# Seven block products for two projections of the second mixture stage

## Chip, cores and metric

The kernel runs on one core of one Trainium2 chip, as one program. The metric is device time in microseconds (us). The kernel before takes 781.18 us (median of three runs, 780.84 to 781.45).

## What is computed

Three parts follow one another on 1536 tokens (2 x 768) of width 512: an attention in which a query sees only keys of its own hash bucket, a mixture in which each token goes through one of eight experts, and a second mixture without experts. The change lies in the last:

```python
def _moe2_ref(x, w_a, w_b, w_out):      # x: 1536 x 512; w_a, w_b: 512 x 1536; w_out: 1536 x 512
    a = x @ w_a
    b = x @ w_b
    return (a * b @ w_out).astype(np.float32)
```

The three weights come as 64-bit floats (the array `w2in`) and are converted to 32 bits on the chip.

## The kernel before

Attention and experts fill the first 465 us. They leave the second stage's input y transposed in SBUF: 512 channels as four blocks of 128 partitions (index d) by 1536 tokens. y is kept as two tiles, `y_h` (rounded to fp32r) and `y_l` (what the rounding left), and weights are split in the same way, so every product of two numbers takes three matmuls: h by h, h by l, l by h (`mm3`).

The stage goes through 1536 hidden units in 12 chunks f of 128, for two halves c of the tokens (768 each), and each half in two steps hf of 384 tokens. The list `steps` has 48 entries (c, f, hf). A step's `ab` (L954) makes a and b in two PSUM banks, `aba` and `abb`: 2 x 4 channel blocks x 3 matmuls, the weights standing, 384 tokens streaming. ScalarE copies a (L965), VectorE multiplies b by it (L966), ScalarE rounds the product to `gh` (L969) and VectorE subtracts to `gl` (L970). `outp` (L975) multiplies `gh` and `gl` by the w_out block: three blocks of 128 tokens, three matmuls of 512 columns each, added up in six PSUM banks `acc0` to `acc5` over the 12 chunks. After the last chunk ScalarE or VectorE copies each bank to an `osb` tile and GpSimd scatters its rows to the output (L420). `outp` runs one step behind `ab`.

The order of the instructions on each engine is the order of the program: everything stands under `tc.manual_schedule()`, there is no planner, each engine takes its own instructions in order, and semaphores make them wait for each other.

Weights: `w2_load` (L802, on SP) brings chunk m as 1.5 MB of raw words; `w2_a` (ScalarE, L488) and `w2_b` (VectorE, L493, L495, L499) convert each third (w_a, w_b, w_out; 512 columns each) to a 32-bit tile `t2`; `w2_c` splits it: h on ScalarE (L826), l on GpSimd (L827). Chunk numbers m run from 0 to 23, the second dozen being the same weights again for the later tokens. Chunks 2 to 9 stay in SBUF as `t2` tiles (the pool `keep`); 0, 1, 10 and 11 are loaded and converted a second time as 12, 13, 22 and 23. `conv_pre` and `conv_post` place this work around each step: before a step the splits for the next one, after it the conversions.

Of the kernel before, what the change touches and what calls it, by code (L numbers as in the profile page):

```python
# [19 lines left out]
S, D, NB, NH = 768, 64, 2, 8  # L20
NT = 6
N, DM, E, FF, F2 = 1536, 512, 8, 1024, 1536
C = 224
KEEP = range(2, 10)
# [9 lines left out]
def attn_moe_kernel(ctx: ExitStack, tc: tile.TileContext, xin, cst, projd, wblk, wmoe, w2in, out):  # L34
    nc = tc.nc
    PE, ACT, DVE, POOL = nc.tensor, nc.scalar, nc.vector, nc.gpsimd

    const = ctx.enter_context(tc.tile_pool(name="const", bufs=1))
    dram = ctx.enter_context(tc.tile_pool(name="dram", bufs=1, space=DRAM))
# [6 lines left out]
    big = ctx_a.enter_context(tc.tile_pool(name="big", bufs=1))  # L46

    cs = const.tile([128, CW], F32, name="cs")
    wb = const.tile([128, NH, 160], F32, name="wb")
    wl = const.tile([128, 80], F32, name="wl")  # L50
    pst = const.tile([128, 64], F32, name="pst")
# [4 lines left out]
    idtab = dram.tile([N, 2], F32, name="idtab")  # L56
    ones = const.tile([128, 128], BF16, name="ones")
    tri = const.tile([128, 128], BF16, name="tri")
    lg = const.tile([128, 12, 16], F32, name="lg")
# [427 lines left out]
    def f64_hi(r, t):  # L487
        ACT.activation(t, r.bitcast(F32)[:, :, 1], ACTF.Copy, scale=float(2.0**-112))  # L488

    def f64_f32(r, t, x, parts=(0, 1, 2)):  # L490
        tu = t.bitcast(U32)
        if 0 in parts:
            DVE.tensor_scalar(out=x, in0=tu, scalar1=0x80000000, scalar2=None, op0=ALU.bitwise_and)  # L493
        if 1 in parts:
            DVE.scalar_tensor_tensor(  # L495
                out=x, in0=r[:, :, 0], scalar=29, in1=x, op0=ALU.logical_shift_right, op1=ALU.bitwise_or
            )
        if 2 in parts:
            DVE.scalar_tensor_tensor(out=tu, in0=tu, scalar=3, in1=x, op0=ALU.logical_shift_left, op1=ALU.bitwise_or)  # L499
# [94 lines left out]
    with tc.manual_schedule():  # L594
# [30 lines left out]
        for n in (2, 1):  # L625
            part, half = half[:n], half[n:]
# [22 lines left out]
            out=tokc.bitcast(I32)[:, :, 0], in0=cs[:, C_TOK:C_TOK + 12], scalar1=-float(E * C), scalar2=None, op0=ALU.add  # L649
# [10 lines left out]
        for g in range(NG):  # L660
            h, t = divmod(g, NT)
# [132 lines left out]

        R2, W2 = {}, {}

        T2, X2, keep = {}, {}, []

        def known(m):
            return m - 12 in KEEP  # L800

        def w2_load(m):  # L802
            if m < 24 and not known(m):
                R2[m] = r2.tile([128, F2, 2], U32, tag="r2", name="r2")
                nc.sync.dma_start(out=R2[m], in_=w2in[m % 12].bitcast(U32).rearrange("p (n two) -> p n two", two=2))

        def w2_a(m, i):
            if m < 24 and not known(m):
                if m in KEEP:
                    T2[m, i] = keep[0].tile([128, 512], F32, tag=f"t{m}{i}", name="t2")  # L810
                else:
                    T2[m, i] = c2.tile([128, 512], F32, tag="t2", name="t2", bufs=6)
                f64_hi(R2[m][:, i * 512:(i + 1) * 512], T2[m, i])

        def w2_b(m, i, parts=(0, 1, 2)):
            if m < 24 and not known(m):
                if 0 in parts:
                    X2[m, i] = c2.tile([128, 512], U32, tag="x2", name="x2")
                f64_f32(R2[m][:, i * 512:(i + 1) * 512], T2[m, i], X2[m, i], parts)

        def w2_c(m, i):
            if m < 24:
                h = s2.tile([128, 512], F32R, tag=f"h2{i}", name=f"h2{i}")
                l = s2.tile([128, 512], F32R, tag=f"l2{i}", name=f"l2{i}")
                t = T2[m - 12 if known(m) else m, i]
                ACT.activation(h, t, ACTF.Copy)  # L826
                POOL.tensor_tensor(out=l, in0=t, in1=h.bitcast(F32), op=ALU.subtract)  # L827
                W2[m, i] = h, l

        XG, HT, Y = {}, {}, {}  # L830

# [115 lines left out]
        ctx_m.close()  # L947
        ctx_w.close()

        keep.append(ctx_2.enter_context(tc.tile_pool(name="keep", bufs=1)))  # L950
# [4 lines left out]
        def ab(c, f, hf):  # L955
            p = [pa.tile([128, 512], F32, tag="ab" + "ab"[i], name="ab" + "ab"[i]) for i in range(2)]
            t0 = c * 768 + hf * 384
            first = (c, f, hf) == (0, 0, 0)
            order = [(i, d) for k in range(2) for i in range(2) for d in (2 * k, 2 * k + 1)]
            for i, d in order if first else sorted(order):  # L960
                    wh, wl = W2[c * 12 + f, i]
                    w = slice(d * 128, (d + 1) * 128)
                    mm3(p[i][:, :384], wh[:, w], wl[:, w], y_h[:, d, t0:t0 + 384], y_l[:, d, t0:t0 + 384], d == 0, d == 3)
# [11 lines left out]
        def outp(c, f, hf):  # L975
            wh, wl = W2[c * 12 + f, 2]
            h, l = G.pop((c, f, hf))
            for j in range(3):
                i = hf * 3 + j
                if f == 0:  # L980
                    acc[i] = pa.tile([128, 512], F32, tag=f"acc{i}", name=f"acc{i}")
                w = slice(j * 128, (j + 1) * 128)
                PE.matmul(acc[i], h[:, w], wh, start=(f == 0), stop=False)
                PE.matmul(acc[i], h[:, w], wl, start=False, stop=False)
                PE.matmul(acc[i], l[:, w], wh, start=False, stop=(f == 11))
                if f == 11:
                    o = gp.tile([128, DM], F32, tag="o", name="osb", bufs=7)
                    k = c * 6 + i
                    if i % 2 == 0:
                        ACT.activation(o, acc.pop(i), ACTF.Copy, scale=cc[:, k:k + 1])  # L990
                    else:
                        DVE.tensor_scalar(out=o, in0=acc.pop(i), scalar1=cc[:, k:k + 1], scalar2=None, op0=ALU.mult)
                    scatter(
                        scat_o, out=out, out_offset=bass.IndirectOffsetOnAxis(ap=ids.bitcast(I32)[:, k, 0:1], axis=0),
                        in_=o, in_offset=None,
                    )

        def conv_pre(m, hf):
            if hf == 0:
                w2_c(m, 2)  # L1000
            else:
                w2_c(m + 1, 0)
                w2_c(m + 1, 1)
# [9 lines left out]
                w2_a(m + 2, 0)  # L1013
                w2_a(m + 2, 1)

        conv = [(m, hf) for m in range(25) for hf in range(2)]
        steps = [(m // 12, m % 12, hf) for m, hf in conv[:48]]
        steps[-3], steps[-2] = steps[-2], steps[-3]
        for n in range(48):
            conv_pre(*conv[n + 1])  # L1020
            ab(*steps[n])
            if n:
                outp(*steps[n - 1])
            conv_post(*conv[n + 1])
        outp(*steps[-1])
        ctx_2.close()
        overflow()

# [57 lines left out]
```

## Time and profile before

| | us |
|---|---|
| median of three runs | 781.18 |
| the profiled execution | 780.29 |
| its span, first to last instruction | 778.5 |
| TensorE busy (matmuls) | 750.7 (96%) |
| weight loads busy (beside matmuls) | 644.4 (83%) |
| VectorE busy | 484.5 (62%) |
| ScalarE busy | 413.0 (53%) |
| GpSimd busy | 229.6 (29%) |
| mean granted TensorE clock | 0.984 |

The profiled execution's time lies 1.8 us above its span and 0.9 us under the median of the runs. Shares of the span are means over stages of different kinds, so they say little about one of them; a stage is read by its own stretch of time. Matmuls overlap: one of 384 columns is on record with 0.34 us, while the next starts 0.175 us later, so starts are compared and not durations. In the rows PE is TensorE, PEld its weight loads, DVE VectorE, ACT ScalarE, POOL GpSimd.

### The profile page before, as it was taken

How to read it: one execution, taken by the hardware profiler on the slowest of the kernel's cores; microseconds unless marked ns; L12 is line 12 of the kernel's file. 1: busy time of each engine (PE TensorE's matmuls, PEld its weight loads, DVE VectorE, ACT ScalarE, POOL GpSimd, SP SyncE). 2: the span in 40 equal slices, each digit the busy share in tenths (PEclk: the TensorE clock that was granted, in tenths of full speed). 3: DMA queues.
4: the chain of work that ended last, by engine and by line, in shares of the span. 5: the costliest groups of instructions: out<-in, count | busy, mean ns of one | idle time of the engine just before them, and what ended most of it. 6: DMA issues, size and time to landing. Idle time of an engine off the chain costs nothing. (4 is left out here: it accounts for less than half of the span.)

```text
span 778.5 us, 13032 instructions
## 1 busy us (share of the span) xinstructions
PE 750.7 (96%) x4911; PEld 644.4 (83%) x4912; DVE 484.5 (62%) x862; ACT 413.0 (53%) x768; POOL 229.6 (29%) x226
## 2 busy tenths in 40 slices
PE   7899999999999989799999999999999999999995
PEld 5566666667666789799999999999999999999995
DVE  5777777788786767466667875666676731111442
ACT  4777777777777435355556654444434432322331
POOL 3223233222534382500000003233333443333223
PEclk8999999999999989899999999999999999999998
DMA  7257241212201055876796552424233430000002
GB/s 241 91 198 254 95 166 56 102 63 69 96 32 59 28 203 180 112 223 216 216 375 216 185 164 82 162 82 162 92 153 111 174 122 1 1 1 1 0 1 84
DMA packets 28916, 94.75 MB, mean 122 GB/s; under 512 B 5984, under 2 KB 9392, under 8 KB 26800
## 3 DMA queue, kind: packets, MB, share of 16 engines
q1 hardware_dynamic: 26176, 87.35, 34.1%
q0 software_dynamic: 2304, 6.31, 2.2%
q8 instruction: 41, 0.67, 0.4%
q10 hardware_dynamic: 368, 0.20, 0.1%
q14 instruction: 27, 0.22, 0.1%
HBM read 79.62 MB, written 13.12 MB: 119 GB/s over the span
## 5 line engine op out<-in xcount | busy, mean ns | idle before, releaser
L827 POOL TENSOR_TENSOR l<-t,h 128x512 fp32r<-128x512 f32 x72 | 95.7, 1334 | 324.9 <-ACT h L826 321.5
L163 DVE TENSOR_REDUCE mm<-s 128x1 f32<-128x768 f32 x96 | 91.8, 956 | 33.9 <-PE s L158 30.3
L474 DVE TENSOR_TENSOR wl<-wr,wh 128x1024 fp32r<-128x1024 f32 x62 | 75.9, 1224 | 53.5 <-ACT wh L473 49.8
L184 PEld LDWEIGHTS tp<-cs,p 128*128 128x128 f32 x576 | 63.1, 142 | 55.4 <-ACT p L171 35.4
L171 ACT ACTIVATE p<-s,sb 128x768 f32<-128x768 f32 x96 | 95.2, 992 | 19.9 <-PE tp L184 10.1
L966 DVE TENSOR_TENSOR a_sb<-abb,a_sb 128x384 f32<-128x384 f32 x48 | 26.8, 558 | 121.8 <-PE abb L858 103.4
L473 ACT ACTIVATE wh<-wr 128x1024 fp32r<-128x1024 f32 x64 | 67.9, 1061 | 57.2 <-PE y L885 49.5
L188 ACT ACTIVATE pt<-tp 128x384 f32<-128x384 f32 x144 | 67.1, 490 | 45.3 <-PE tp L184 44.1
L826 ACT ACTIVATE h<-t 128x512 fp32r<-128x512 f32 x72 | 44.4, 629 | 87.0 <-DVE t L499 80.5
L184 PE MATMUL tp<-cs,p 128*128 128x128 f32 x576 | 84.2, 283 | 6.4 <-ACT p L171 4.6
L157 PE MATMUL s<-tk,tq 76*128 76x384 f32 x192 | 73.7, 384 | 2.3 <-DVE tq L134 2.3
L856 PE MATMUL h<-xh,wh 128*128 128x224 f32 x256 | 72.9, 285 | 2.5 <-ACT wh L473 1.5
L885 PE MATMUL y<-hl,wh 128*128 128x224 f32 x256 | 72.1, 282 | 2.1 <-DVE hl L870 2.1
L858 PE MATMUL h<-xh,wl 128*128 128x224 f32 x256 | 71.5, 279 | 2.6 <-DVE wl L474 2.3
L884 PE MATMUL y<-hh,wh 128*128 128x224 f32 x256 | 71.7, 280 | 1.2 <-ACT hh L869 1.2
L857 PE MATMUL h<-xl,wh 128*128 128x224 f32 x256 | 71.3, 279 | 0.3 <-DVE xl L411 0.3
L886 PE MATMUL y<-hh,wl 128*128 128x224 f32 x256 | 71.2, 278 | 0.0
L199 PE MATMUL av<-pt,v 128*64 128x384 f32 x360 | 71.1, 503 | 0.0
L158 PE MATMUL s<-bk,bq 128*128 128x384 f32 x192 | 65.5, 341 | 0.0
L856 PE MATMUL aba<-y_h,h 128*128 128x384 f32 x192 | 65.0, 339 | 0.3 <-ACT a_sb L965 0.3
L856 PE MATMUL abb<-y_h,h 128*128 128x384 f32 x192 | 65.1, 339 | 0.0
L857 PE MATMUL aba<-y_l,h 128*128 128x384 f32 x192 | 64.5, 336 | 0.2 <-DVE y_l L892 0.2
(161 smaller groups left out, 1789.4 us busy)
## 6 DMA issues: line engine op xcount, KB each, us to landing
wr<-wmoe SPq DMA_DIRECT2D x64, 512.0 KB
r<-w2in SPq DMA_DIRECT2D x16, 1536.0 KB
x<-xin SPq DMA_DIRECT2D x30, 384.0 KB
xr<-zero SPq DMA_DIRECT2D x13, 512.0 KB
xg<-xr SPq DMA_DIRECT2D x14, 256.0 KB
v<-xin SPq DMA_DIRECT2D x16, 192.0 KB
wb<-wblk SPq DMA_DIRECT2D x1, 640.0 KB
x<-xin SPq DMA_DIRECT2D x3, 192.0 KB
```

The source lines that it names most:

```text
L157: PE.matmul(p[:, c, :384], T[h, 0][:76, qs], T[h, 1][:76, sl], start=True, stop=False)
L163: DVE.tensor_reduce(out=m[:, 1:2], in_=st[g][:, :, :384], axis=AX.XY, op=ALU.min)
L171: ACT.activation(p.rearrange("p (c n) -> p c n", c=2), st.pop(g)[:, :, :384], ACTF.Exp, scale=scl.pop(g), bias=nbs.pop(g), accum_out=sums[ ...
L184: PE.transpose(ps[:, j * 128:(j + 1) * 128], pt_[g][:, k * 128:(k + 1) * 128], ident)
L474: eng.tensor_tensor(out=l, in0=r, in1=h.bitcast(F32), op=ALU.subtract)
L827: POOL.tensor_tensor(out=l, in0=t, in1=h.bitcast(F32), op=ALU.subtract)
L856: PE.matmul(ps, wh, xh, start=first, stop=False)
L857: PE.matmul(ps, wh, xl, start=False, stop=False)
L858: PE.matmul(ps, wl, xh, start=False, stop=last)
L884: PE.matmul(p, wh[:, w], h, start=(f == 0 and d % 2 == 0), stop=False, skip_group_check=True)
L885: PE.matmul(p, wh[:, w], l, start=False, stop=False, skip_group_check=True)
L886: PE.matmul(p, wl[:, w], h, start=False, stop=(f == 7), skip_group_check=True)
```

## The change

For the later tokens (c = 1) and chunks 0 to 10, `seven` takes the place of four `ab`-like groups of products. It takes a and b of both token halves as one product of 2 x 2 blocks. The weight blocks are A11, A12 (w_a, lower and upper 256 channels) and A21, A22 (w_b); the blocks of y are its lower and upper 256 channels by two groups of 384 tokens. Seven products of sums and differences of blocks replace eight products of blocks. Each of the seven has two channel blocks x 3 = 6 matmuls of 384 columns.

- The sums and differences of y (t1 to t4, with h and l: `TH`, `TL`) are made once by `t_work`, in six portions on VectorE and ScalarE in steps 17 to 22 of the earlier half.
- The sums and differences of the weights (s1 to s4) are made by `s_work` on VectorE, one chunk ahead. `part` and `piece` split each of the seven weight operands (128 x 256): h on ScalarE, l on GpSimd.
- The products go to the two banks by turns. Between them, `fill` places one third of an `outp` of the chunk before, and `side` the next chunk's weight work. Copies and sums of banks (p1, u2, c11, u3, c22, c21, c12) are on ScalarE and VectorE.
- The last chunk runs `ab` and `outp` as before, in another order: `ab`, what is pending, `ab`, both `outp`.
- The pool `keep` goes. `w2_b` stores each converted tile to DRAM (`w32`, on SP's queue), and `t2_load` reads the tiles back for chunks 12 to 23. Nothing is converted twice.
- In the earlier half w_a and w_b are split in pieces of 256 columns instead of 512.
- `osb` has 5 buffers instead of 7; three small tiles move to another pool.

```diff
-        def known(m):
-            return m - 12 in KEEP
...
+        def t2_load(m):
+            if m < 24:
+                for i in range(3):
+                    nc.sync.dma_start(out=t2_tile(m, i), in_=w32[m - 12][:, i * 512:(i + 1) * 512])
...
         def w2_b(m, i, parts=(0, 1, 2)):
-            if m < 24 and not known(m):
+            if m < 12:
                 if 0 in parts:
                     X2[m, i] = c2.tile([128, 512], U32, tag="x2", name="x2")
                 f64_f32(R2[m][:, i * 512:(i + 1) * 512], T2[m, i], X2[m, i], parts)
+                if 2 in parts:
+                    nc.sync.dma_start(out=w32[m][:, i * 512:(i + 1) * 512], in_=T2[m, i])
...
+        def piece(key, src):
+            p = s2.tile([128, 2, 256], F32R, tag="pc", name="pc", bufs=11)
+            ACT.activation(p[:, 0], src, ACTF.Copy)
+            POOL.tensor_tensor(out=p[:, 1], in0=src, in1=p.bitcast(F32)[:, 0], op=ALU.subtract)
+            PCS[key] = p
...
+            return [
+                [whole(t3, lo_d, n2), whole(t1, lo_d, n1)],
+                [tt(t1, t3, t1), whole(t2, hi_d, n2)],
+                [tt(t3, t2, t3), tt(t2, t2, t1), hi(2)],
+                [tt(t4, yh[:, hi_d, n1], t2), tt(t4, t4, yl[:, hi_d, n1], ALU.add), hi(1), hi(0)],
+                [low(2), low(1), hi(3)],
+                [low(0), low(3)],
+            ]
...
+            if k == 0:
+                DVE.tensor_tensor(out=new("s1"), in0=a_part(m, "21"), in1=a_part(m, "22"), op=ALU.add)
+                DVE.tensor_tensor(out=new("s2"), in0=SW["s1"], in1=a_part(m, "11"), op=ALU.subtract)
+            elif k == 1:
+                DVE.tensor_tensor(out=new("s3"), in0=a_part(m, "11"), in1=a_part(m, "21"), op=ALU.subtract)
+            else:
+                DVE.tensor_tensor(out=new("s4"), in0=a_part(m, "12"), in1=SW["s2"], op=ALU.subtract)
+
+        ORDER = ("11", "s2", "12", "s3", "s1", "22", "s4")
...
+            def finish(hf, a, b):
+                DVE.tensor_tensor(out=b, in0=a, in1=b, op=ALU.mult)
...
+                ACT.activation(h, b, ACTF.Copy)
+                DVE.tensor_tensor(out=l, in0=b, in1=h.bitcast(F32), op=ALU.subtract)
+                G[1, f, hf] = h, l
+
+            x, y = bank(0), bank(1)
+            product(x, m, "11", *y_part(lo_d, n1), True)
+            p1 = sb("p1")
+            ACT.activation(p1, x, ACTF.Copy)
+            fill(0)
+            side(0)
+            product(y, m, "s2", TH[1], TL[1], True)
+            u2 = add(sb("u2"), y, p1)
+            fill(1)
+            side(1)
+            product(x, m, "12", *y_part(hi_d, n1), False)
+            c11 = sb("c11")
+            ACT.activation(c11, x, ACTF.Copy)
+            fill(2)
+            side(2)
+            product(y, m, "s3", TH[2], TL[2], False)
+            u3 = add(sb("u3"), y, p1)
+            fill(3)
+            side(3)
+            x = bank(0)
+            product(x, m, "s1", TH[0], TL[0], True)
+            c22 = add(sb("c22"), x, u3)
+            fill(4)
+            side(4)
+            product(y, m, "22", TH[3], TL[3], False)
+            c21 = add(sb("c21"), y, p1)
+            finish(0, c11, c21)
+            fill(5)
+            side(5)
+            product(x, m, "s4", *y_part(hi_d, n2), False)
+            c12 = add(sb("c12"), x, u2)
+            finish(1, c12, c22)
+            side(6)
...
+            def side(k):
+                if k == 0:
+                    w2_c(m, 2)
+                if f < 10:
+                    if k < 3:
+                        s_work(m + 1, k)
+                    part(m + 1, ORDER[k])
...
+                if k == 6:
+                    t2_load(m + 2)
...
+        w2_c(23, 2)
+        ab(1, 11, 0)
+        while pend:
+            outp(*pend.pop(0))
+        ab(1, 11, 1)
+        outp(1, 11, 0)
+        outp(1, 11, 1)
```

## Rows read from the trace of the kernel before

**Rows 1.** Busy time in two stretches of one chunk each, the first in the earlier half of the stage, the second in the later. Columns: stretch and its length in us, then busy us (and instructions) of PE, PEld, DVE, ACT and POOL, the granted clock, the DMA share and GB/s.

```profile
527.57:540.10 12.53, 12.53 (x68) 11.78 (x67) 8.37 (x13) 5.41 (x10) 3.99 (x4) 1.00 0.35 127
664.54:677.07 12.53, 12.53 (x68) 11.78 (x67) 2.24 (x4) 3.72 (x7) 3.81 (x3) 1.00 0.00 1
```

**Rows 2.** Instructions in order of time, TensorE, from the matmuls of `aba` to those of the next step. Columns here and in all rows in order of time: start us, duration us, engine, line, operation, output and inputs, shape; in brackets the idle time before it and who ended it.

```profile
655.27 0.33 PE L856 MATMUL aba<-y_h,h 128*128 128x384 f32 x1
655.27 0.19 PEld L857 LDWEIGHTS aba<-y_l,h 128*128 128x128 f32 x1
...
655.44 0.34 PE L857 MATMUL aba<-y_l,h 128*128 128x384 f32 x1
...
657.37 0.34 PE L856 MATMUL abb<-y_h,h 128*128 128x384 f32 x1
...
659.47 0.39 PE L983 MATMUL acc<-h,gh 128*128 128x512 f32 x1
...
661.54 0.33 PE L856 MATMUL aba<-y_h,h 128*128 128x384 f32 x1
```

**Rows 3.** In order of time: ScalarE's copy of `aba` and the first matmul that writes the bank again, at step 20 to 21 and at the start of the later half.

```profile
597.22 0.47 ACT L965 ACTIVATE a_sb<-aba 128x384 f32<-128x384 f32 x1
...
598.30 0.33 PE L856 MATMUL aba<-y_h,h 128*128 128x384 f32 x1
...
623.29 0.47 ACT L965 ACTIVATE a_sb<-aba 128x384 f32<-128x384 f32 x1
...
623.82 0.45 PE L856 MATMUL aba<-y_h,h 128*128 128x384 f32 x1 [0.29 <-ACT a_sb L965]
...
624.10 0.34 PE L857 MATMUL aba<-y_l,h 128*128 128x384 f32 x1
```

**Rows 4.** In order of time: at 474 and 654 operations that follow one another on one engine without needing each other, at 659 and 660 what follows the last matmul of a step.

```profile
474.38 0.56 DVE L970 TENSOR_TENSOR gl<-a_sb,gh 128x384 fp32r<-128x384 f32 x1 [0.59 <-ACT gh L969]
...
474.85 0.42 DVE L493 TENSOR_SCALAR x<-t 128x512 uint32<-128x512 uint32 x1
...
654.07 0.53 ACT L969 ACTIVATE gh<-a_sb 128x384 fp32r<-128x384 f32 x1 [2.22 <-DVE a_sb L966]
...
654.50 1.14 ACT L826 ACTIVATE h<-t 128x512 fp32r<-128x512 f32 x2
...
659.30 0.34 PE L858 MATMUL abb<-y_h,l 128*128 128x384 f32 x1
...
659.74 0.56 DVE L966 TENSOR_TENSOR a_sb<-abb,a_sb 128x384 f32<-128x384 f32 x1 [4.55 <-PE abb L858]
...
660.33 0.53 ACT L969 ACTIVATE gh<-a_sb 128x384 fp32r<-128x384 f32 x1 [2.22 <-DVE a_sb L966]
...
660.90 0.56 DVE L970 TENSOR_TENSOR gl<-a_sb,gh 128x384 fp32r<-128x384 f32 x1 [0.59 <-ACT gh L969]
```

**Rows 5.** Groups of instructions by line and shape: the two operations on 256 columns. Columns: line, engine, operation, tiles, shapes, count, busy us, mean ns, idle time before.

```profile
L368 POOL TENSOR_TENSOR xh<-x_all,xh 128x256 fp32r<-128x256 f32 x1 | 0.7, 737 | 0.4 <-ACT xh L367 0.4
L367 ACT ACTIVATE xh<-x_all 128x256 fp32r<-128x256 f32 x1 | 0.4, 421 | 3.4 <-DVE x_all L247 3.4
```

**Rows 6.** In order of time: VectorE and GpSimd side by side, at three places.

```profile
425.43 1.22 DVE L474 TENSOR_TENSOR wl<-wr,wh 128x1024 fp32r<-128x1024 f32 x1 [0.22 <-ACT wh L473]
...
426.00 1.80 POOL L827 TENSOR_TENSOR l<-t,h 128x512 fp32r<-128x512 f32 x1 [102.30 <-ACT h L826]
...
426.57 1.78 DVE L495 SCALAR_TENSOR_TENSOR x<-r,x 128x512 uint32<-128x512 uint32 x1
...
606.37 0.63 ACT L826 ACTIVATE h<-t 128x512 fp32r<-128x512 f32 x1 [1.92 <-DVE t L499]
...
606.71 0.69 DVE L495 SCALAR_TENSOR_TENSOR x<-r,x 128x512 uint32<-128x512 uint32 x1
...
607.08 1.47 POOL L827 TENSOR_TENSOR l<-t,h 128x512 fp32r<-128x512 f32 x1 [3.62 <-ACT h L826]
...
607.50 1.60 DVE L499 SCALAR_TENSOR_TENSOR t<-t,x 128x512 uint32<-128x512 uint32 x1
...
609.90 1.29 POOL L827 TENSOR_TENSOR l<-t,h 128x512 fp32r<-128x512 f32 x1 [1.35 <-ACT h L826]
...
610.24 0.56 DVE L966 TENSOR_TENSOR a_sb<-abb,a_sb 128x384 f32<-128x384 f32 x1 [1.14 <-ACT a_sb L965]
```

**Rows 7.** In order of time: the end of the program, from the last step's `outp` to the last scatters.

```profile
766.00 0.39 PE L983 MATMUL acc<-h,gh 128*128 128x512 f32 x1
...
766.87 0.53 ACT L969 ACTIVATE gh<-a_sb 128x384 fp32r<-128x384 f32 x1 [2.22 <-DVE a_sb L966]
...
768.95 0.75 DVE L992 TENSOR_SCALAR osb<-acc,cc 128x512 f32<-128x512 f32 x1 [0.96 <-PE acc L985]
...
769.63 0.69 ACT L990 ACTIVATE osb<-acc,cc 128x512 f32<-128x512 f32 x1 [2.23 <-PE acc L985]
...
769.98 0.96 POOL L420 DMA_INDIRECT out<-osb,ids  x1 [4.37 <-DVE osb L992]
...
772.50 0.96 POOL L420 DMA_INDIRECT out<-osb,ids  x1 [0.19 <-POOLq L504]
```

More of the change, by code (lines that the diff above doesn't have):

```diff
@@ L56, in attn_moe_kernel @@
     idtab = dram.tile([N, 2], F32, name="idtab")
+    w32 = [dram.tile([128, F2], F32, name=f"w32_{m}") for m in range(12)]
     ones = const.tile([128, 128], BF16, name="ones")
@@ L973, in attn_moe_kernel, with outp @@
         acc = {}
-        def outp(c, f, hf):
+        def outp(c, f, hf, js=range(3)):
             wh, wl = W2[c * 12 + f, 2]
-            h, l = G.pop((c, f, hf))
-            for j in range(3):
+            h, l = G[c, f, hf]
+            for j in js:
                 i = hf * 3 + j
@@ L1014, in conv_post @@
                 w2_a(m + 2, 1)
[L1016 to L1021, printed above, removed]
+        TH, TL = ([fast.tile([128, 2, 384], F32R, name=f"t{n}{i}") for i in range(4)] for n in "hl")
+        n1, n2 = slice(768, 1152), slice(1152, N)
+        lo_d, hi_d = slice(0, 2), slice(2, 4)
@@ new lines, in t_work, with whole, tt, hi @@
+        def t_work():
+            yh, yl = y_h.bitcast(F32), y_l.bitcast(F32)
+            t1, t2, t3, t4 = TF = [fast.tile([128, 2, 384], F32, name=f"tf{i}") for i in range(4)]
+            def whole(o, d, n):
+                return lambda: DVE.tensor_tensor(out=o, in0=yh[:, d, n], in1=yl[:, d, n], op=ALU.add)
+            def tt(o, x, y, op=ALU.subtract):
+                return lambda: DVE.tensor_tensor(out=o, in0=x, in1=y, op=op)
+            def hi(i):
+                return lambda: ACT.activation(TH[i], TF[i], ACTF.Copy)
+            def low(i):
+                return lambda: DVE.tensor_tensor(
+                    out=TL[i], in0=TF[i], in1=TH[i].bitcast(F32), op=ALU.subtract
+                )
+            return [
[6 more added lines that the diff above has]
+            ]
@@ new lines, in attn_moe_kernel, with part, product @@
+        ORDER = ("11", "s2", "12", "s3", "s1", "22", "s4")
+        def part(m, nm):
+            piece((m, nm), SW[nm] if nm in SW else a_part(m, nm))
+        def product(ps, m, nm, xh, xl, start):
+            p = PCS.pop((m, nm))
+            for j in range(2):
+                wh, wl = (p[:, k, j * 128:(j + 1) * 128] for k in range(2))
+                x_h, x_l = xh[:, j], xl[:, j]
+                PE.matmul(ps, wh, x_h, start=start and j == 0, stop=False, skip_group_check=True)
+                PE.matmul(ps, wh, x_l, start=False, stop=False, skip_group_check=True)
+                PE.matmul(ps, wl, x_h, start=False, stop=(j == 1), skip_group_check=True)
@@ new lines, in y_part, with seven, bank, sb @@
+        def y_part(d, n):
+            return y_h[:, d, n], y_l[:, d, n]
+        def seven(f, fill, side):
+            m = 12 + f
+            tags = ("aba", "abb") if f % 2 == 0 else ("abb", "aba")
+            def bank(k):
+                return pa.tile([128, 512], F32, tag=tags[k], name=tags[k])[:, :384]
+            def sb(nm):
+                return fast.tile([128, 384], F32, tag=nm, name=nm)
+            def add(o, ps, x):
+                DVE.tensor_tensor(out=o, in0=ps, in1=x, op=ALU.add)
+                return o
+            def finish(hf, a, b):
+                DVE.tensor_tensor(out=b, in0=a, in1=b, op=ALU.mult)
+                h = gp.tile([128, 384], F32R, tag="gh", name="gh")
+                l = gp.tile([128, 384], F32R, tag="gl", name="gl")
+                ACT.activation(h, b, ACTF.Copy)
[34 more added lines that the diff above has]
+            side(6)
@@ L1022, in attn_moe_kernel @@
+        conv = [(m, hf) for m in range(13) for hf in range(2)]
+        todo = t_work()
+        for n in range(24):
+            if n < 22:
+                conv_pre(*conv[n + 1])
+            elif n == 22:
+                for k in range(3):
+                    s_work(12, k)
+                for nm in ORDER[:4]:
+                    part(12, nm)
+            else:
+                for nm in ORDER[4:]:
+                    part(12, nm)
+            ab(0, n // 2, n % 2)
             if n:
-                outp(*steps[n - 1])
+                outp(0, (n - 1) // 2, (n - 1) % 2)
@@ L1024, in attn_moe_kernel, with fill @@
             conv_post(*conv[n + 1])
-        outp(*steps[-1])
+            if n in (19, 23):
+                t2_load(12 + (n == 23))
+            if 17 <= n < 23:
+                for g in todo.pop(0):
+                    g()
+        pend = [(0, 11, 1, (j,)) for j in range(3)]
+        for f in range(11):
+            m = 12 + f
+            def fill(k):
+                if pend:
+                    outp(*pend.pop(0))
[6 more added lines that the diff above has]
+                    part(m + 1, ORDER[k])
+                elif k in (1, 4):
+                    w2_c(23, k // 4)
+                if k == 6:
+                    t2_load(m + 2)
+            seven(f, fill, side)
+            while pend:
+                outp(*pend.pop(0))
+            pend = [(1, f, hf, (j,)) for hf in range(2) for j in range(3)]
```

63 lines of the change are left out of this document (38 added, 25 removed).

## The prediction

> **What bounds the kernel now.** I read the clock first, then the busy time in stretches, then single instructions in order of time; the chain of waits holds only the last scatter, so it can't tell what bounds this stage. In the second mixture stage TensorE is busy 12.53 of 12.53 us at clock 1.00, both where weights are converted and where they are not [rows 1]; VectorE, ScalarE and GpSimd have room. The reader is to see in the order of time that matmuls start evenly: twelve of 384 columns take 655.27 to 657.37, 0.175 each, nine of 512 take 659.47 to 661.54, 0.23 each [rows 2]. A step is 24 x 0.175 + 9 x 0.23 = 6.27, a chunk of weights (two steps) 12.54. So time is won only by fewer matmuls, and lost only where TensorE is made to wait.
>
> **What the change takes away.** For eleven chunks of the later tokens, a and b cost 7 products of 6 matmuls instead of 8: 66 matmuls fewer, 66 x 0.175 = 11.55 us. The conversions of weights 12, 13, 22, 23 go too; they cover nothing on the path, except that TensorE waits once for ScalarE's copy at 623.82, and the second matmul starts 0.28 instead of 0.175 after the first: 0.29 + 0.1 = 0.4 us [rows 3].
> [...]
>
> **A chunk of seven products, if nothing waits.** A product is 6 x 0.175 = 1.05 us, a fill (three matmuls of 512) 0.69. Counted from the first matmul of the chunk, the products start at 0, 1.74, 3.48, 5.22, 6.96, 8.70 and 10.44 and end at 11.49; 12.54 - 11.49 = 1.05 is the saving of one chunk. Each hand-over from the rows: product's end to copy 0.27 (659.30 + 0.175 to 659.74), VectorE's multiply to ScalarE's h 0.59, h to VectorE's l 0.57 [rows 4]; an independent operation starts 0.43 after a ScalarE h and 0.47 after a VectorE l [rows 4]; 256 columns take 0.42 on ScalarE and 0.74 on GpSimd [rows 5], about 0.43 on VectorE (0.56 for 384 and 1.22 for 1024 [rows 4, 6] give 1.03 ns a column).
> The tight place is the end of a chunk. "22" ends at -1.74. c21 starts at -1.47, the multiply at -0.88, h at -0.29, l at 0.28. c12 has its product at 0.27 but stands behind l on VectorE: 0.75. Its multiply starts at 1.34, h at 1.93, l at 2.50, ending 3.06. On ScalarE, where each operation starts 0.1 before the one ahead has ended (0.53 against 0.43), the part of "s4" follows h at 2.36, p1 at 2.68 (0.47 [rows 3], needed at 3.48: in time), then w_out's h at 3.05 to 3.68 (0.63 [rows 6]). Next on VectorE come s1 (from 2.97), s2, and only then u2, for which the fourth product waits at 5.22. Undisturbed, s1, s2, u2 end at 3.40, 3.85, 4.3: in time by 0.9.
>
> **The wait I expect.** VectorE and GpSimd get in each other's way. GpSimd asked at 426.00 while VectorE's L474 ran to 426.65, took 1.80 instead of 1.29, and went before the next VectorE operation, which started at 426.57 and ended at 428.35, 0.55 after GpSimd; 607.08 and 607.50 show the same. An operation with one input in PSUM keeps its 0.56 under a running GpSimd (610.24 beside 609.90) [rows 6]. u2 and c12 are of that sort; s1, s2 and the l's are not.
> GpSimd's subtraction for "s4" is ready 0.08 after its ScalarE half (607.00 to 607.08 [rows 6]): 2.36 + 0.42 + 0.08 = 2.86. l lets go about 0.15 before its end, at 2.91, before s1 is there at 2.97. So GpSimd runs to 3.65, s1 ends 0.28 later at 3.93, and w_out's l, ready at 3.76, goes before s2, which needs s1: 3.78 to 5.07. s2 ends at 5.35, u2 starts 0.09 before that and ends at 5.82. TensorE starts 0.05 after the release (623.76 to 623.82) and loses 0.1 on the second matmul [rows 3]: 5.82 + 0.05 + 0.1 - 5.22 = 0.75. Queued behind u2 are s3, s4 and u3, needed 3 us later. The end of the next chunk is the same again, so it recurs in chunks 1 to 9 (chunk 0 has no l ahead, chunk 10 has no s1): 9 x 0.75 = 6.7 us. Bounds: 0, if s1 gets in first; 9 x (0.75 + 0.74) = 13.4, if one more part's subtraction goes ahead of s1 or s2.
>
> **Hand-over in the earlier half.** In a pair of steps VectorE has 12.53 - 8.37 = 4.16 us idle [rows 1]. The sums and differences of y add four operations of 768 columns, 1.22 - 256 x 1.03 ns = 0.96 each, 3.84, before any waiting for GpSimd. I take VectorE 1.2 late at the end of step 19's conversion (bounds 0 and 2.6, two GpSimd operations of 1.29 [rows 6]). ScalarE's copy after that conversion ends at 597.69 and TensorE needs it at 598.30 [rows 3]: 0.6 spare. There the change queues on ScalarE, ahead of the copy, the rounding of t3, which waits for one more VectorE operation (0.96) and takes 0.84 (256 and 512 columns take 0.42 and 0.63), and behind it four weight parts instead of the one operation of before: 4 x 0.32 - 0.53 = 0.75. 1.2 + 0.96 + 0.84 + 0.75 - 0.6 = 3.1 us, once; bounds 1.9 and 4.5.
>
> **The end.** The old-style step after chunk 10 starts on the bank that c12 reads until 1.31, with no fill left between: 1.4 us, once. And six blocks close in the last 4.1 us instead of three. The first copy stands behind h on ScalarE (0.87 + 0.43 after the last step's a and b) and takes 0.69; the scatter follows 0.28 later (769.70 to 769.98), at 2.27; six at 1.26 each end at 2.27 + 5 x 1.26 + 0.96 = 9.5, where three ended 773.46 - 766.00 = 7.46 [rows 7]: 2.1 us. Bounds 0.8 (one scatter less late) and 3 (the sixth copy waits for one of five buffers).
>
> **Costs taken at nothing.** Smaller weight parts in the first half (four GpSimd operations of 0.74 for two of 1.29): GpSimd has 3.99 of 12.53 busy; uncovered, 4 x 0.74 - 2 x 1.29 = 0.4 a chunk. Stores to DRAM add half of what is loaded to a DMA share of 0.35 [rows 1]; on SP each waits for a conversion that the next load waits for anyway. A reload is issued a chunk ahead, some 7 us before its first use; what these cost uncovered is rival 3.
>
> **Sum.** -11.55 - 0.4 + 6.7 + 3.1 + 1.4 + 2.1 = +1.35 on the profiled execution's 780.29 (span 778.5 and 1.8 around it): 781.6. That execution lies 0.9 below the median of 781.18, so I forecast 782.5. A measurement here can't tell less than 0.2%, 1.56 us, from no change: same is 779.6 to 782.7.
>
> **Rivals.** (1) s1 gets in ahead of the "s4" subtraction. Then s1, s4's part, s2 and u2 end at 3.40, 4.00, 4.29 and 4.76, w_out's l comes after s2, and no chunk waits: 782.5 - 6.7 = 775.8. For it: the margin is 2.97 - 2.86, and 0.42 on ScalarE rests on a single row. Against it: GpSimd went first in both cases of [rows 6]. [...]
> (2) GpSimd falls behind, and its operations also stand before the multiply and l of c21. Then l, c12, h, p1 all come 0.74 later, p1 ends at 3.9, and the third product waits 0.5 as well as the fourth 0.97: 1.47 a chunk, 782.5 - 6.7 + 9 x 1.47 = 789. It decides from 1.05 a chunk, where the saving is gone. Against it: GpSimd's 7 x 0.74 + 1.29 = 6.5 fits into 12.2.
> (3) The weights don't come back from DRAM in time and chunks wait for s1's input. At 1 us a chunk: 792 (10 chunks). Against it: 7 us of lead, and the stage's DMA share falls to nothing in the later half [rows 1].
>
> **Chances.** The forecast 0.50 (own range 780 to 785.5: faster 0.07, same 0.20, slower 0.23); rival 1 0.35, all faster; rival 2 0.11 and rival 3 0.04, slower. Faster 0.42, same 0.20, slower 0.38. The range reaches down to rival 1 with the least hand-over cost, 775.8 - 1.2 = 774.6, say 774.5, and up to waits of 1.1 a chunk with a little more at the hand-over, 786.5; above it lie rivals 2 and 3.
>
> **What will show it.** In a chunk of seven products: the time from one "11" to the next (11.5 or 12.2), TensorE waiting for u2's line before the fourth product, s2 with about 1.4 instead of 0.43 under w_out's subtraction; TensorE idle for some 3 us behind ScalarE near 598; six scatters in a row at the end. The prediction is wrong if chunks run at 11.5 without a wait, or if waits stand at another product.

## The result, and the profile after

The changed kernel takes 794.35 us (median of 13 runs, 785.73 to 798.5), the kernel before in the same comparison 781.18 (13 runs, 779.21 to 790.55): 1.0123 times as long, 95% interval 1.008 to 1.0167. The forecast was 782.5, the range up to 786.5. The runs of either kernel are spread over 11 to 13 us, so below only medians of one comparison are set against each other, and the parts are read from profiles.

The profiled execution took 796.35 (span 794.5, mean clock 0.972). Of its page, TensorE's busy time; it is 4.3 us less than before, in a span 16.0 us longer:

```profile
PE 746.4 (94%) x4845; PEld 634.3 (80%) x4846; DVE 538.0 (68%) x937; ACT 420.3 (53%) x841; POOL 277.8 (35%) x307
```

Cut at the second matmul of the mixture stage (468.85 before, 481.01 after; the first one starts earlier in both and the second waits for y's low half), the 16.0 us are: ahead of the stage 10.9, the wait at its second matmul 1.48 instead of 0.25, so 1.2 more, and from there to the end 313.5 instead of 309.65, 3.8 more. Two thirds of the difference lie ahead of everything that the prediction spoke of.

**Ahead of the stage.** VectorE and GpSimd in order of time in the changed kernel, at the start of the expert stage, where GpSimd zeroes `y_h` and `y_l` with eight instructions back to back:

```profile
281.69 6.07 POOL L783 MEMSET y_h<- 128x1760 f32 x4 [2.09 <-DMA xr<-x_all,pos_i]
...
283.48 10.34 DVE L432 CAST noff_i<-noff 128x16 int32<-128x16 f32 x1
...
287.71 6.08 POOL L783 MEMSET y_l<- 128x1760 f32 x4
```

The conversion `noff_i` works on 128 x 16 numbers; alone it takes 0.17 (below). Here it took 10.34: it began during the second zeroing and came to an end with the last (287.71 + 6.08 = 293.79). The kernel before has the same instructions; there the conversion got in behind the second zeroing, and a later small operation waited 3.45, until the last had ended (293.58):

```profile
283.29 1.25 DVE L432 CAST noff_i<-noff 128x16 int32<-128x16 f32 x1
...
290.16 3.45 DVE L345 TENSOR_SCALAR rt_s<-rt_s 128x4 f32<-128x4 f32 x1
```

What that does to TensorE, in stretches (length, busy us and matmuls, granted clock, DMA share, GB/s), first the changed kernel, then the kernel before:

```profile
284.00:288.00 4.00, 1.68 (x8) 0.50 0.74 258
288.00:292.00 4.00, 0.00 (x0) 0.50 0.09 37
292.00:296.00 4.00, 1.61 (x7) 0.50 0.00 0
```

```profile
284.00:288.00 4.00, 4.00 (x20) 0.50 0.79 284
288.00:292.00 4.00, 4.00 (x33) 0.86 0.57 199
```

TensorE waited 8.7 us for the one low half that stood behind `noff_i` on VectorE, and its clock stayed at 0.50 through the whole of it (284 to 296 above). In the kernel before it waited 1.25 for the low half that stood behind the small operation of 3.45. TensorE in order of time, first the changed kernel, then the kernel before:

```profile
294.39 0.56 PE L900 MATMUL y<-hl,wh 128*128 128x224 f32 x1 [8.70 <-DVE hl L885]
```

```profile
294.35 0.37 PE L885 MATMUL y<-hl,wh 128*128 128x224 f32 x1 [1.25 <-DVE hl L870]
```

**A chunk of seven products** (chunk 2), all engines in order of time; it answers to [rows 1, 6]:

```profile
655.63 0.34 PE L1093 MATMUL aba<-y_h,pc 128*128 128x384 f32 x1
...
658.59 0.81 POOL L830 TENSOR_TENSOR pc<-s,pc 128x256 fp32r<-128x256 f32 x1 [1.49 <-PE abb L1095]
...
658.72 0.97 DVE L1076 TENSOR_TENSOR s<-t 128x256 f32<-128x256 f32 x1
...
659.49 1.34 POOL L842 TENSOR_TENSOR l<-t,h 128x512 fp32r<-128x512 f32 x1
...
659.72 1.40 DVE L1077 TENSOR_TENSOR s<-s,t 128x256 f32<-128x256 f32 x1
...
661.04 0.54 DVE L1111 TENSOR_TENSOR u<-abb,p 128x384 f32<-128x384 f32 x1
...
661.64 0.44 PE L1093 MATMUL abb<-th,pc 128*128 128x384 f32 x1 [0.61 <-DVE u L1111]
...
668.07 0.34 PE L1093 MATMUL abb<-y_h,pc 128*128 128x384 f32 x1
```

Counted from 655.63, the "s4" part starts on GpSimd at 2.96 (worked out: 2.86), w_out's at 3.86 (3.78), s2 takes 1.40 (1.4), the fourth product starts at 6.01 (5.87: u2's end at 5.82 and 0.05). The next chunk starts 12.44 later. Without a wait it is 11.56 (e3, below), so the wait costs 0.88: 0.77 up to the fourth product's first matmul, and 0.11 up to its second (worked out: 0.75 with both).

**The start of the stage.** SP stores the last converted weights, then loads `ids`; VectorE multiplies `cc` from it, and y's low half stands behind that:

```profile
472.57 3.88 SPq L823 DMA_DIRECT2D w<-t  x2
...
477.08 0.38 SPq L915 DMA_DIRECT2D ids<-idtab  x1
...
479.11 0.41 PE L871 MATMUL aba<-y_h,pc 128*128 128x384 f32 x1
...
479.71 0.17 DVE L916 TENSOR_TENSOR cc<-ids 128x12 f32<-128x12 f32 x1 [2.51 <-DMA ids<-idtab]
...
480.24 1.16 DVE L907 TENSOR_TENSOR y_l<-y,y_h 128x448 f32 x2 [0.36 <-ACT pc L829]
...
481.01 0.41 PE L872 MATMUL aba<-y_l,pc 128*128 128x384 f32 x1 [1.48 <-DVE y_l L907]
```

The kernel before issued the load of `ids` at 453.20, behind no store.

**The hand-over.** ScalarE rounds t3 (L1047), splits four weight parts, and only then copies the bank that TensorE waits for; it answers to [rows 3], 14.1 later in time, of which 12.2 had been lost by the second matmul of the stage and 1.9 are this stall:

```profile
608.89 1.95 DVE L1044 TENSOR_TENSOR tf<-tf,tf 128x768 f32<-128x768 f32 x2
...
609.88 0.85 ACT L1047 ACTIVATE th<-tf 128x768 fp32r<-128x768 f32 x1 [4.62 <-DVE tf L1044]
...
610.63 1.32 ACT L829 ACTIVATE pc<-t 128x256 fp32r<-128x256 f32 x4
...
611.86 0.47 ACT L980 ACTIVATE a_sb<-aba 128x384 f32<-128x384 f32 x1
...
612.38 0.44 PE L871 MATMUL aba<-y_h,pc 128*128 128x384 f32 x1 [1.75 <-ACT a_sb L980]
```

**The end**, to set beside [rows 7]:

```profile
768.22 0.44 PE L871 MATMUL aba<-y_h,pc 128*128 128x384 f32 x1 [1.23 <-DVE c L1111]
...
780.85 0.39 PE L998 MATMUL acc<-h,gh 128*128 128x512 f32 x1
...
783.09 0.99 POOL L420 DMA_INDIRECT out<-osb,ids  x1 [11.76 <-ACT osb L1005]
...
789.44 0.96 POOL L420 DMA_INDIRECT out<-osb,ids  x1 [0.19 <-POOLq L504]
```

From the first `outp` matmul of the last step to the end of the last scatter's issue it is 9.55 (790.40 - 780.85) instead of 7.46, 2.1 more; to the end of the span it is 13.65 (794.5 - 780.85) instead of 12.5 (778.5 - 766.00), only 1.1 more. Behind that issue 4.1 us pass instead of 5.1; no run shows why.

### The profile page after: what moved, and what is told of

Its sections match the earlier page's. It is cut to its first block, busy times and chain, and to the rows that moved or that the text cites. A ratio compares the mean times of both kernels' runs of the same rounds, so it can differ in the third digit from the quotient of the medians.

```text
span 794.5 us, 13394 instructions
## 1 busy us (share of the span) xinstructions
PE 746.4 (94%) x4845; PEld 634.3 (80%) x4846; DVE 538.0 (68%) x937; ACT 420.3 (53%) x841; POOL 277.8 (35%) x307
## 5 line engine op out<-in xcount | busy, mean ns | idle before, releaser
L830 POOL TENSOR_TENSOR pc<-t,pc 128x256 fp32r<-128x256 f32 x85 | 77.8, 934 | 206.8 <-ACT pc L829 206.8
L474 DVE TENSOR_TENSOR wl<-wr,wh 128x1024 fp32r<-128x1024 f32 x62 | 76.0, 1226 | 60.3 <-ACT wh L473 57.0
L900 PEld LDWEIGHTS y<-hl,wh 128*128 128x128 f32 x256 | 50.9, 199 | 9.9 <-DVE hl L885 9.8
L999 PE MATMUL acc<-l,gh 128*128 128x512 f32 x144 | 56.8, 395 | 0.0
L1000 PE MATMUL acc<-h,gl 128*128 128x512 f32 x144 | 56.5, 392 | 0.1
L998 PE MATMUL acc<-h,gh 128*128 128x512 f32 x144 | 56.4, 392 | 0.0
L842 POOL TENSOR_TENSOR l<-t,h 128x512 fp32r<-128x512 f32 x24 | 32.7, 1362 | 63.8 <-ACT h L841 63.0
```

The costliest lines, as they stand in the source:

```text
L474: eng.tensor_tensor(out=l, in0=r, in1=h.bitcast(F32), op=ALU.subtract)
L830: POOL.tensor_tensor(out=p[:, 1], in0=src, in1=p.bitcast(F32)[:, 0], op=ALU.subtract)
L900: PE.matmul(p, wh[:, w], l, start=False, stop=False, skip_group_check=True)
```

## Experiments

They were run in three comparisons, e1 to e4, e5 to e8 and e9 to e12, each on a chip of its own together with the kernel before, whose medians there were 774.76, 781.16 and 775.29. "Stage" is the time from the second matmul of the mixture stage to the end of the span of the profiled execution (the wait at that matmul lies ahead of it): 309.65 before, 313.5 after.

**e1 and e2: the eight zeroings spread out** ("paced" in the expectations), in the kernel before and in the changed one.

```diff
-        for y in (y_h, y_l):
-            for d in range(4):
-                POOL.memset(y.bitcast(F32)[:, d], 0.0)
...
-            DVE.scalar_tensor_tensor(
+            hl = DVE.scalar_tensor_tensor(
                 out=l, in0=p[:, :C], scalar=0.0, in1=h.bitcast(F32), op0=ALU.max, op1=ALU.subtract
             )
+            if e == 0:
+                after(POOL.memset((y_h, y_l)[f // 4].bitcast(F32)[:, f % 4], 0.0), [hl.ins])
```

> The kernel before, its eight GpSimd zeroings of y_h and y_l each tied to the low half of a hidden tile of the first expert, so that they no longer run back to back. Theory (the spread of the runs, and 11 us of the profiled difference, come from VectorE's conversion noff_i losing boundary after boundary between the eight zeroings): the noff_i conversion lasts at most one zeroing (under 1.6 us), all runs lie within 2 us of each other, near the lowest level of the kernel before (779). Rival (the upper levels of the kernel before have another cause): the runs still spread from 779 to 788.

> The changed kernel with the same edit. Theory: the runs close up at the lowest level of the changed kernel, 785 to 787, so 6 to 8 us above e1: that is the price of the change itself, and the rest of its 13 us is the lost boundaries. Rival (the change itself slows the expert stage): still 792 to 797, 13 to 17 above e1, with TensorE's idle time in the expert stage as before the edit.

e1: 765.39 (765.05 to 769.56), 0.9886 of the kernel before (0.9852 to 0.992). e2: 772.82 (769.17 to 778.1), 0.9975 (0.9949 to 1.0001). The first four zeroings still ran in a row, from 281.53 in e1, their hidden tiles being done by then; `noff_i` took 0.17 in both because it came before them (0.17 to 0.18 in e9 to e11, where the zeroings are spread out as here). So this pair doesn't test the part of the theory on `noff_i`; the operation that met the zeroings was `rt_s`, 1.58 in both and 1.59 to 1.60 in e9 to e11 (with the zeroing as it was it took 7.61 in e12). The runs drew together, to 4.5 and 9 us, not to 2. On this chip, then, the zeroing as it was costs the kernel before some 9 us in its usual run, and with it spread out the change costs 7.4.

**e3: u2 ahead of s1 and s2** on VectorE, on top of e2.

```diff
             u2 = add(sb("u2"), y, p1)
+            if f < 10:
+                s_work(m + 1, 0)
             fill(1)
...
-                    if k < 3:
+                    if 0 < k < 3:
                         s_work(m + 1, k)
```

> e2, and in each chunk of seven products VectorE's u2 is queued ahead of s1 and s2 of the chunk after instead of behind them. Theory (TensorE waits at the fourth product for u2, which stands behind s1 and s2 on VectorE, and these wait for GpSimd's part subtraction and w_out's): the idle time of 0.61 at the fourth product and the 1.83 in chunk 1 go, the spacing from one first product to the next falls from 12.4 to about 11.6, the time by 7 to 9 us, to about 778. Rival (the wait comes back at another product, for the parts that s1 and s2 make come 0.6 later): the spacing stays over 12.2 and the time within 3 us of e2.

762.58 (761.59 to 767.22): 10.2 below e2, stage 305.6 instead of 314.8. In order of time, VectorE and GpSimd in a chunk, and the first matmul of this chunk and the next:

```profile
651.21 0.34 PE L1092 MATMUL aba<-y_h,pc 128*128 128x384 f32 x1
...
654.50 0.56 DVE L1110 TENSOR_TENSOR u<-abb,p 128x384 f32<-128x384 f32 x1
...
654.97 0.42 DVE L1075 TENSOR_TENSOR s<-t 128x256 f32<-128x256 f32 x1
...
655.06 1.48 POOL L839 TENSOR_TENSOR l<-t,h 128x512 fp32r<-128x512 f32 x1
...
655.42 1.40 DVE L1076 TENSOR_TENSOR s<-s,t 128x256 f32<-128x256 f32 x1
...
662.76 0.34 PE L1092 MATMUL abb<-y_h,pc 128*128 128x384 f32 x1
```

s2 still takes 1.40 under w_out's subtraction, but nothing waits behind it now: 11.55 from chunk to chunk, from chunk 2 on. Chunk 0 gets a wait of 0.6 at the sixth product, and chunk 1 still lasts 12.9. Of the 9.2 that the stage gained, 1.5 are the clock, which had fallen in e2's chunk 1 (last section) and didn't here.

**e4: roundings later and the end reordered**, on top of e3.

```diff
-                [tt(t3, t2, t3), tt(t2, t2, t1), hi(2)],
-                [tt(t4, yh[:, hi_d, n1], t2), tt(t4, t4, yl[:, hi_d, n1], ALU.add), hi(1), hi(0)],
-                [low(2), low(1), hi(3)],
-                [low(0), low(3)],
+                [tt(t3, t2, t3), tt(t2, t2, t1)],
+                [hi(2), tt(t4, yh[:, hi_d, n1], t2), tt(t4, t4, yl[:, hi_d, n1], ALU.add)],
+                [hi(1), hi(0), hi(3), low(2)],
+                [low(1), low(0), low(3)],
...
+        for _ in range(3):
+            outp(*pend.pop(0))
         ab(1, 11, 0)
-        while pend:
-            outp(*pend.pop(0))
         ab(1, 11, 1)
         outp(1, 11, 0)
+        while pend:
+            outp(*pend.pop(0))
         outp(1, 11, 1)
```

(The last step's `gh` and `gl` then lie in `TH[0]` and `TL[0]`.)

> e3, and two more edits: the roundings of t1 to t4 go one half-chunk later, behind their inputs (the 1.75 stall of TensorE near 612 should go), and at the end three output products of chunk 10 come ahead of the first ordinary half-chunk, the output products of the first half of chunk 11 ahead of the other three of chunk 10 (the 1.23 wait at 768 goes, three scatters are issued earlier). Theory: 1.75 + 1.2 + about 2 of tail, so some 4 to 5 us below e3, near 773, which is below the kernel before. Rival (these waits are hidden by later ones): within 1.5 us of e3.

760.61 (759.46 to 762.6): 2.0 below e3, stage 302.0 instead of 305.6. Both stalls are gone, but part of it came back: the low halves are later now, and in chunk 0 TensorE waits 1.2 at the sixth product where it waited 0.6, and 0.5 once in chunk 1.

**e5 and e6: both kernels again, unchanged, and e7: only the three small tiles moved.**

```diff
-    wb = const.tile([128, NH, 160], F32, name="wb")
-    wl = const.tile([128, 80], F32, name="wl")
-    pst = const.tile([128, 64], F32, name="pst")
+    wb = big.tile([128, NH, 160], F32, name="wb")
+    wl = big.tile([128, 80], F32, name="wl")
+    pst = big.tile([128, 64], F32, name="pst")
```

> The kernel before, unchanged, for a second profile. Theory (VectorE's small conversions lose the boundaries between GpSimd's zeroings, differently in each run): its times spread over some 10 us again, and its profile shows noff_i or rt_s lasting several us between 281 and 294, and the second matmul of the mixture stage some 8 to 11 us later than the 458 of e1. Rival (the first profile's stalls in the expert stage belong to that one execution or chip): noff_i as short as in e1 (0.2) and the stage begins near 458.

> The changed kernel, unchanged, beside e5. Theory: above e5 by the 7 us that e2 stood above e1, plus or minus what the zeroing does in either: 4 to 14 us. Rival (the change makes the zeroing's stall worse than before, every time): 12 to 14 again, with noff_i at 8 us or more.

> The kernel before with only wb, wl and pst taken from the pool that the changed kernel takes them from: the one edit of the change that lies ahead of the expert stage and alters addresses there. Theory (the addresses have nothing to do with it): the same times as e5 within its spread. Rival (they have): 6 us or more above e5.

e5: 781.17 (779.12 to 792.21). e6: 788.66 (783.01 to 794.36), 7.5 above e5. e7: 781.88 (777.53 to 790.23), 1.0009 of the kernel before (0.997 to 1.0048), so the addresses of these tiles don't explain the 13 us; at most 4 us could be theirs. VectorE in order of time, first e5 and then e6; the roles of the first profiles are exchanged, and the second matmul of the stage came at 474.95 in e5, 17 after e1's 458.05 where 8 to 11 was expected, and at 466.26 in e6:

```profile
282.71 10.28 DVE L432 CAST noff_i<-noff 128x16 int32<-128x16 f32 x1
```

```profile
281.83 1.28 DVE L432 CAST noff_i<-noff 128x16 int32<-128x16 f32 x1
...
288.70 3.50 DVE L345 TENSOR_SCALAR rt_s<-rt_s 128x4 f32<-128x4 f32 x1
```

The long conversion belongs to neither kernel. Still the changed kernel had its longer times more often. The times of each kernel fall into a shorter and a longer group with a gap of 2.6 to 5.5 us between: in the longer group lie 10 of 13 in the first comparison and 8 of 12 here, of the kernel before 5 of 13 and 4 of 12. Why is open.

**e8: w_out's split behind the fourth product**, on top of e2, with u2 left behind s1 and s2.

```diff
-                if k == 0:
-                    w2_c(m, 2)
                 if f < 10:
                     if k < 3:
                         s_work(m + 1, k)
                     part(m + 1, ORDER[k])
-                elif k in (1, 4):
+                if k == 3:
+                    w2_c(m, 2)
+                if f == 10 and k in (1, 4):
```

> The paced changed kernel of e2, with w_out's split put behind the fourth product instead of ahead of s1 and s2. [...] Rival (it is the order alone: u2 stands behind s1 and s2 whatever they last): the wait stays, within 2 us of e2.

The wait meant is TensorE's 0.61 at the fourth product. I expected it to go, s2 to fall from 1.40 to about 0.43, and the time to fall by 5 to 8 us against e2's 772.8.

779.31 (777.16 to 783.38), 0.9963 of the kernel before (0.9932 to 0.9994). On this chip even the spread-out zeroing left the expert stage disturbed (in 310 to 330, after the last zeroing, TensorE was busy 14.7 of 20 us), so the time says little against e2's on another chip; the stage does: 309.1 instead of 314.8, or instead of 313.3 without the clock's fall in e2. In order of time, VectorE in a chunk, and the first matmul of this and of the next:

```profile
669.75 0.34 PE L1092 MATMUL aba<-y_h,pc 128*128 128x384 f32 x1
...
672.83 0.97 DVE L1075 TENSOR_TENSOR s<-t 128x256 f32<-128x256 f32 x1
...
673.84 0.84 DVE L1076 TENSOR_TENSOR s<-s,t 128x256 f32<-128x256 f32 x1
...
681.65 0.34 PE L1092 MATMUL abb<-y_h,pc 128*128 128x384 f32 x1
```

s2 takes 0.84 instead of 1.40, TensorE is idle for 0.06 instead of 0.61 ahead of the fourth product, and the chunk lasts 11.90 instead of 12.44. s2 didn't fall to 0.43, for the next weight part's subtraction takes w_out's place ahead of it (673.48 to 674.40, and s2 ends 0.28 later). The wait is made on GpSimd, then, and its order decides how much of it is left.

**e9 to e12: the load of `ids` ahead of the stores, and what all the edits bring.** e9 is e4 with this edit, e11 is e2 with it alone, e10 is e1 once more, e12 is e9 with the zeroing as it was.

```diff
-            (7, 3): [lambda: w2_c(0, 2), lambda: w2_load(2), lambda: w2_b(1, 0, (0, 1))],
+            (7, 3): [ids_load, lambda: w2_c(0, 2), lambda: w2_load(2), lambda: w2_b(1, 0, (0, 1))],
...
-            (7, 7): [ids_load],
```

> e4 with the load of ids issued earlier, ahead of the stores of the converted weights instead of behind them on SP's queue. Theory (the changed kernel's SP queue holds ids back behind stores that wait for VectorE's conversions; the multiplication cc on VectorE then waits for ids, the last low half y_l stands behind cc, and TensorE waits 1.4 to 1.5 at the second matmul of the mixture stage): that wait falls to about 0.25 as in the kernel before, and the mixture stage lasts about 301 against 309.7 of the kernel before; the time 5 to 9 us below e10. Rival: the wait is hidden by a later one, and the time stays within 3 us of e10.

> The paced kernel before (e1 once more), for a comparison with e9, e11 and e12 on one chip. Theory: no conversion longer than one zeroing, and a median several us below the kernel before as it was (9 in the first comparison). Rival: the gain of the first comparison belonged to that chip, and here it is within 2 us of the kernel before.

> e2 with only the load of ids moved ahead of the stores. Theory: the wait at the second matmul of the mixture stage falls from 1.4 to about 0.25, nothing else moves; the stage from there on lasts 314.8 as in e2, and against e10 the time is 6 us higher (e2 was 7.4 above e1). Rival: the wait stays, for another reason than the ids load.

> The changed kernel with u2 first, the roundings later, the end reordered and ids earlier, and the eight zeroings as they were. Theory (the change's own waits cost 9 to 10 us and its fewer matmuls bring 10 to 11, while the zeroing is a matter of chance in both kernels): against the kernel before, as it was, 6 to 9 us faster in the median, with a spread of some 10 us left. Rival (the changed kernel loses more to the zeroing than the kernel before does): not faster by more than 3 us.

| | median us | of the kernel before (95%) | stage |
|---|---|---|---|
| e9 | 758.04 | 0.9789 (0.977 to 0.9809) | 302.5 |
| e10 | 766.03 | 0.9884 (0.9865 to 0.9903) | 310.1 |
| e11 | 771.20 | 0.9949 (0.9935 to 0.9964) | 313.4 |
| e12 | 766.17 | 0.9876 (0.9841 to 0.9911) | 302.1 |

e11 lies 5.2 above e10 and e9 8.0 below it. The waits of TensorE in e9 show both that `ids` was the cause and the longest of the edits' own stalls that is left (engine, line, waited for: us in total, times, longest):

```profile
PE abb L1094 <- DVE u L1112: 1.2, 1, 1.2
...
PE aba L869 <- DVE y_l L906: 0.2, 1, 0.2
```

e12 beats the kernel before by 9.1 with the zeroing untouched, and stays 8.1 above e9 on the same chip, from which it differs by the zeroing alone. In its profile `noff_i` came ahead of the zeroing, and the next operation of that kind paid; VectorE in order of time, first e12 and then e9:

```profile
280.10 0.17 DVE L432 CAST noff_i<-noff 128x16 int32<-128x16 f32 x1
...
285.83 7.61 DVE L345 TENSOR_SCALAR rt_s<-rt_s 128x4 f32<-128x4 f32 x1
```

```profile
284.33 1.59 DVE L345 TENSOR_SCALAR rt_s<-rt_s 128x4 f32<-128x4 f32 x1
```

## Why the prediction was wrong

**The sum was +1.35; the changed kernel's own price is 5 to 7.** From the mixture stage on, its first wait included, the profiled pair differs by 5.1. With the zeroing spread out the medians differ by 7.4 (e2 over e1), and by 5.2 when `ids` no longer waits (e11 over e10). Part of the 7.4 can be the clock's fall in chunk 1, 1.5 in e2's profile; the rest above 5.1 isn't placed. That e6 over e5 gives 7.5 as well doesn't confirm it, for there the zeroing acts in both: the shorter groups of their runs lie 2.8 apart, those of the first comparison 6.8. On top of 781.18 the price gives 786.3 to 788.6, the upper end of the range or above it, and the longer runs come on top of that. The terms for the profiled pair, measured between the starts of matmuls, so that a late second matmul is counted:

| term | predicted | measured | from |
|---|---|---|---|
| 66 matmuls fewer | -11.55 | -10.7 | 11 x (12.53 - 11.56) |
| stall at 623.82 goes | -0.4 | -0.6 | 0.45 ahead of its first matmul, 0.11 behind it |
| wait at the fourth product | +6.7 | +9.1 | 8 x 0.88, and 2.1 in chunk 1 |
| chunk 1 ahead of that wait | 0 | +0.8 | 14.48 - 11.56 = 2.9, less 2.1 |
| hand-over | +3.1 | +2.0 | 1.9 at 612.38, and 0.1 on the next start |
| the same, two steps on | 0 | +0.3 | 0.24 at 625.27, and 0.1 on the next start |
| bank of c12 | +1.4 | +1.5 | 1.4 at 768.22, and 0.1 on the next start |
| six scatters | +2.1 | +1.1 | 13.65 - 12.5, to the end of the span |
| the load of `ids` | 0 | +1.2 | 1.48 - 0.25 at 481.01 |

They add up to +4.7 of the 5.1; 0.4 isn't placed. Two terms were 1 us too high each, which hid part of what the others were too low.

- The matmuls: right in kind. The schedule without a wait was worked out as 11.49; it is 11.56.
- The wait at the fourth product: the chain and the place were right, every step to 0.15 us; e3 and e8 show it by two different edits, and rival 1 (s1 gets in first) falls. The term "9 x 0.75" was too small in two ways. It is 0.88 in chunks 2 to 9. And chunk 1 isn't like the others: between 631.8 and 642.4 GpSimd issues six scatters of the earlier half, its subtractions are late, l, c12 and p1 come later and hold up the second and third product (0.8 in all), s2 took 2.07 and TensorE waited 1.83 (rows below). I had taken chunks 1 to 9 as equal; rival 2, GpSimd behind, holds for this one. The 0.15 by which VectorE's l "lets go" before its end is an estimate from [rows 6]: the two GpSimd subtractions that stood beside VectorE's L474 and L495 ended at 427.80 and 608.55, so at 1.29 each they began at 426.51 and 607.26, 0.14 ahead of the ends of those two. In chunk 2 it is 0.14 again (659.40 - 0.74, and l's end at 658.80).
- The hand-over: right place and chain, mis-sized. The step "VectorE 1.2 late" failed: the conversion ended 0.3 late (608.98, before 596.56 + 12.16), t3's subtraction followed it at once, and the lower bound of 1.9 is what happened. "Once" failed too: at 625.27 the copy stood behind four weight parts again, for which s2 was late on VectorE, behind the low halves of t.
- The end: the bank of c12 within 0.1 us. The scatters were issued as worked out, but the sum took the end of their issue for the end of the span, which came 1.1 later and not 2.1.
- "On SP each waits for a conversion that the next load waits for anyway": this step failed. The next load at one place was `ids`, which waits for no conversion; held back behind two stores it cost 1.2 (e11: 0.2 left of the wait once it goes ahead). I had counted the stores' traffic and not what stands behind them in the queue.
- Rival 3 falls: TensorE waited for no reload, and e9 runs with all 36 of them.
- What no step held is the expert stage. The sum starts from 780.29 and so puts the change of the first 465 us at nothing, without a reason: I took them for a constant, the three runs of before (within 0.6 us) for the spread, and 0.2% for what a measurement can tell, where the interval of the result reaches 0.4% to either side. Its trace had the sign: a conversion and a scalar operation on a handful of numbers, 1.25 and 3.45 us long, with TensorE's clock at 0.50 in 284 to 288 (rows above). 10.9 of the 16.0 us of the profiled pair lie there, 8.7 of them in one wait; in the medians it is what the price leaves of the 13, some 6 to 8.

VectorE and GpSimd in order of time in chunk 1 of the changed kernel, and the fourth product's first matmul:

```profile
646.59 2.07 DVE L1077 TENSOR_TENSOR s<-s,t 128x256 f32<-128x256 f32 x1
...
647.12 1.25 POOL L842 TENSOR_TENSOR l<-t,h 128x512 fp32r<-128x512 f32 x1
...
649.18 0.44 PE L1093 MATMUL aba<-th,pc 128*128 128x384 f32 x1 [1.83 <-DVE u L1111]
```

Beside the zeroings, which only write, VectorE's two-input L474 kept its 1.23 (at 281.71 in the changed kernel, a zeroing running from 281.69), while the cast and the `tensor_scalar` were held (10.34, and 3.45 in the kernel before; alone each takes 0.17). Beside GpSimd's subtractions s1 and s2 were held too: 0.97 and 1.40 in chunk 2, where in e3 s1 took 0.42, begun before the subtraction. What makes the difference no run shows.

Open: why the changed kernel meets the long outcome more often, and why TensorE lost time between 310 and 330 in the first profiles (busy 16.10 of 20 us before, 17.53 after) and in e5 to e8 and not in the other two comparisons. Neither was tried. In those same profiles `noff_i` fell into the zeroing, and in the other two comparisons it came ahead of it, with the zeroing as it was (e12) as well as spread out; so what spreading it out brings in the first case is not measured (in e8 `noff_i` met a zeroing with a pause behind it and took 1.34, and the second matmul of the stage still came at 471.77, later than e6's 466.26).

## What to carry to other kernels

Before a small difference is forecast, look in the trace for casts and `tensor_scalar` operations on a few numbers that last several us beside a run of GpSimd instructions (here 3.45 to 10.34 instead of 0.17): that stretch belongs to no edit (`noff_i` took 1.25 and 10.28 in two executions of the kernel before). On the two chips where it was measured, spreading the run out brought the kernel before 9 us (1.2%), about as much as the seven products brought once most of their waits were mended (8.0, e9 under e10). When products get fewer and operands more, price the helpers' order: putting what the next product needs ahead of what the next chunk needs took 9.2 us off the stage here (e3; 1.5 of them the clock). And price a store added to a queue by the first load behind it that doesn't need the same data (here `ids`, 1.2 us).

## What was not expected of the hardware

In these profiles a cast or `tensor_scalar` on VectorE that met the zeroings on GpSimd didn't always get in when one of them ended. Where they follow at once, one every 1.51, it got in at the first boundary (1.25 before, 1.26 in e7, 1.28 in e6) or at none, until the last one had ended (3.45 before, 3.50 in e6, 3.82 in e7, 7.61 in e12, 10.28 in e5, 10.34 after; in e5 282.71 + 10.28 = 292.99, the zeroings' end being 292.95). The same program gave 1.25 in one execution and 10.28 in another. In chunk 2 s1 and s2 ended 0.29 behind the end of one subtraction each, as the prediction worked it out (0.28); but 10.34 spans seven zeroings, and chunk 1's s2 (from 646.59) lasted beyond the end of one subtraction, at 647.14, over the whole of the next, to 648.37.

Behind an idle time of 1.83 e2 lost 1.5 us more. In the first profile of the changed kernel TensorE's clock stayed at 1.00 through chunk 1's wait; in e2, behind the same wait, it fell (length, busy us and matmuls, granted clock, DMA share, GB/s):

```profile
622.00:625.00 3.00, 1.46 (x5) 0.80 0.52 159
625.00:628.00 3.00, 3.00 (x13) 0.63 0.30 90
```

Matmuls of 384 columns then started every 0.32 instead of 0.175, and the chunk lasted 15.98 instead of 14.48. It was so in e6 as well (15.97, with the clock at 0.57 in 636 to 640), and not in e11 (14.48, with an idle time of 1.83 again).
